# A linear-attention and two-MLP kernel: first token block multiplied in whole fp32, its weights split one block later, its bonus sums taken on TensorE

## The chip, the cores and the metric

One core of one Trainium2 chip. The metric is the device time of one execution in microseconds. Three runs of the kernel before gave 975.14, 975.26 and 977.88 us; the median is 975.26 us.

## What is computed

A linear attention with a decaying state runs over 4 batches, 8 heads, 768 tokens and a head size of 48. Two MLPs (384 to 2048 to 384) follow over all 3072 tokens.

```python
for t in range(S):
    cur = einsum('bhd,bhe->bhde', u * k[t], v[t])
    y[t] = einsum('bhd,bhde->bhe', r[t], state + cur)
    state = w[t][..., None] * state + einsum('bhd,bhe->bhde', k[t], v[t])
x = y as (B*S, 384)
h = x @ w_in;  g = h * clip(h + 3, 0, 6) / 6;  x = g @ w_out       # first MLP
h = x @ w2_in; g = h / (1 + exp(-h));          out = g @ w2_out    # second MLP
```

The weights arrive as 8-byte floats, the rest as 4-byte floats. The part `u * k[t]` of the sum is the bonus: for each token and head it comes to the number sum(r*u*k), by which v[t] is multiplied.

## The kernel before

**Tiling.** The 768 tokens of each batch are cut into 6 chunks of 128. A group is one chunk of one batch, so there are 24 groups, and groups 0 to 3 are the first chunk. A block is one chunk of all 4 batches, 512 tokens. The first MLP takes the blocks in turn (`block1(j)`), then the second does (`block2(j)`). The 2048 hidden features are taken in 16 slices of 128 (`fc`).

**A group of attention** (`attention(g)`). VectorE makes running products of the decay in both directions (`pre`, `suf`), multiplies r and k by them (`rh`, `kh`), and TensorE takes the scores in fp32 (`pa`). VectorE masks them (`a`), TensorE turns `kh` (`pk`), ScalarE copies it (`khn`), and TensorE adds up the outputs in fp32 (`py`) and the growth of the state (`pkv`). For the bonus r, k and v come a second time in natural layout (`nat`, tokens on partitions). L642 and L645 multiply r, u and k into `ruk`, L649 sums it for each head into `bb`, and L658 and L663 scale v into `bv`, which L693 adds to `py`. For groups 0 to 3 VectorE does L642 and L645, and for the others GpSimd. ScalarE copies `py` to `xh`, and VectorE takes what that rounding left as `xl` (L703). The state is copied from `pkv` (L730) and multiplied by the decay over the chunk (L734).

**Weights** (`load_w`). Each `fc` is loaded in 8-byte form (`raw`, two buffers, which also take the decay of groups 2 and 3). VectorE turns it into fp32 in three steps (L32, L38, L44 into `bits`), ScalarE rounds it to the upper part (L495), and VectorE takes the rest as the lower part (L496).

**A product of 128x128 by 128x512** is three matmuls in the faster, less exact form of fp32, called fp32r: upper with upper, upper with lower, lower with upper. `mm1` (L784) does this for three input chunks, `mm2` (L797) for three output chunks, so one `fc` of a block has 6 such products or 18 matmuls, and a block has 96 products. Between them ScalarE and VectorE make `g` (L827, L829) and split it into `gh` (L807 or L808) and `gl` (L810).

**Order.** Every operation is handed to a planner with an engine, a price in ns and a key. The planner goes through time: at each engine it takes what can start first, and among these the smallest key. A buffer of a tag is given out in the order in which the tag's buffers were named. The program then runs each engine in that order. Chunk 0 has keys about -100, the attention of chunk j+1 has those of block j, so it is worked off beside block j. Weight tiles (tag `w`, 16 of them) also serve as temporaries of groups 1 to 3 (called `spare` in the trace).

Of the kernel before, what the change touches and what calls it, by code (L numbers as in the profile page):

```python
# [363 lines left out]
def tile_decay_attention_mlp2(  # L364
# [10 lines left out]
):  # L375

# [63 lines left out]
    u_bc = Part(ap_.tile([128, H, D], F32, name="u_bc"))  # L440
    stray = Part(stray_t)
# [31 lines left out]
    wts = {}  # L473

    def load_w(layer, fc, key, where="wp", after=()):
        src = (m1, m2)[layer]
        nm = f"{layer}_{fc}"
        raw = Part(new("cst", "raw", 2, [128, 2, DM, WW], f"raw{nm}", I32))
        op({"SP": 470}, key - 3, lambda e: e.dma_start(
            out=raw.ap.rearrange("p a f t -> p (a f t)"), in_=src[fc]  # L480
        ), writes=[raw], data=1150.0 * WW, after=after)
        if WW == 2:
            bits = Part(new("cst", "bits", 1, [128, 2, DM], f"bits{nm}", I32))
            val = Part(bits.buf, lambda t: t.bitcast(F32))
# [23 lines left out]
        "a0": (2, 0), "a1": (2, NP * C),  # L508
# [3 lines left out]
    def att(tag, shape, g, sub="", bufs=1):  # L512

        if not (0 < g < B and tag + sub in SPARE):
            return Part(new("ap", tag, bufs, shape, f"{tag}{sub}_{g}"))
        i, off = SPARE[tag + sub]
        if (g, i) not in spare:
            spare[g, i] = new("wp", "w", 16, [128, 4 * DM], f"spare{g}_{i}")
# [12 lines left out]
        return Part(spare[g, i], view)  # L531
# [9 lines left out]
    def load_group(g, key):  # L541
        first = 2 <= g < B

        def home(tag, shape, first_home):
            if not first:
                return Part(new("np", tag, 1 if tag == "rk" else 2, shape, f"{tag}{g}"))
            where, t, bufs, size = first_home
            buf = new(where, t, bufs, [128, size], f"{tag}{g}")
            n = 1
            for x in shape[1:]:  # L550
                n *= x
            return Part(buf, lambda t: t[:shape[0], 0:n].rearrange(
                "p (a b) -> p a b", b=shape[2]) if len(shape) == 3 else t[:shape[0], 0:n])

        ws = home("ws", [PD, SEQ + 1], ("cst", "raw", 2, 4 * DM))
        rk = home("rk", [PD, 2 * NP, C], ("wp", "w", 16, 4 * DM))
        nat = home("nat", [128, 2 * H * D + NP * ED], ("wp", "w", 16, 4 * DM))
        for p, src, data in ((ws, wseq_in, 600.0), (rk, rk_in, 1150.0), (nat, nat_in, 1750.0)):
# [4 lines left out]
        return ws, rk, nat  # L563
# [7 lines left out]
    def attention(g, key):  # L571
# [3 lines left out]
        ws, rk, nat = loads.pop(g) if g in loads else load_group(g, key - 2)  # L575
# [3 lines left out]

        def heads(i):  # L580
            return nat.ap[:, i * H * D:(i + 1) * H * D].rearrange("p (h d) -> p h d", d=D)

        def v():
            return nat.ap[:, 2 * H * D:].rearrange("p (a e) -> p a e", e=ED)
# [45 lines left out]
        if not last:  # L630
# [11 lines left out]
        op({"POOL": 1000} if not first else {"DVE": 560}, key, lambda e: e.tensor_tensor(  # L642
            ruk.ap, heads(0), u_bc.ap, op=ALU.mult
        ), [nat, u_bc], [ruk], port=True)
        op({"POOL": 1000} if not first else {"DVE": 560}, key, lambda e: e.tensor_tensor(  # L645
            ruk.ap, ruk.ap, heads(1), op=ALU.mult
        ), [ruk, nat], [ruk], port=True)
        bb = Part(new("ap", "bb", 2, [128, H, 1], f"bb{g}"))
        op({"DVE": 540}, key, lambda e: e.tensor_reduce(  # L649
            flat(bb), ruk.ap, axis=AX.X, op=ALU.add  # L650
        ), [ruk], [bb])
# [3 lines left out]
        def bonus(e):  # L655
            b = bb.ap.rearrange("p (a i) x -> p a i x", i=2)
            x = v()
# [11 lines left out]
        op({"DVE": 740}, key, bonus, [nat, bb], [bv], port=True)  # L669
# [4 lines left out]
        def outputs(e):  # L674
            x = v()
# [23 lines left out]
           [*a_sb, nat, bv, ident] + ([rh, state] if state else []), [py])  # L699
        xh, xl = x_parts[0, j]  # L700
        sl = slice(o * C, (o + 1) * C)
        op({"ACT": 490}, key, lambda e: e.activation(xh.ap[:, :, sl], py.ap, AF.Copy), [py], [xh])
        op({"DVE": 560}, key, lambda e: e.tensor_tensor(  # L703
            xl.ap[:, :, sl], py.ap, xh.ap[:, :, sl].bitcast(F32), op=ALU.subtract
        ), [py, xh], [xl])

        if not last:
            pkv = att_ps([PD, NP, ED], "pkv", g)

            def outer_kv(e):  # L710
                for p in range(NP):
                    e.matmul(pkv.ap[:, p, :], khn.ap[:, p, :], v()[:, p, :], start=True, stop=True)  # L712

            op({"PE": 700}, key, outer_kv, [khn, nat], [pkv])
# [13 lines left out]
            def first_state(e):  # L728
                for a, b in DENSE:
                    e.tensor_copy(now.ap[:, :, b], pkv.ap[:, :, a])  # L730

            op({"DVE": 760}, key, add_state if state else first_state,
               [pkv, now] if state else [pkv], [now])
            op({"DVE": 560}, key, lambda e: e.tensor_tensor(  # L734
                now.ap.rearrange("p a (i e) -> p a i e", e=T),
                now.ap.rearrange("p a (i e) -> p a i e", e=T),
                grown.ap.to_broadcast([PD, NP, NB, T]), op=ALU.mult,
            ), [now, grown], [now], port=True)
# [33 lines left out]
    def new_x(layer, j):  # L772
        x_parts[layer, j] = tuple(
            Part(new("xp", f"x{i}", 2, [128, KC, N], f"x{i}_{layer}_{j}", F32R)) for i in range(2)
        )

    def mm1(layer, j, fc, key):
        xh, xl = x_parts[layer, j]
        wh, wl = wts[layer, fc]
        h = Part(new("ps", "h", 2, [128, N], f"h{layer}_{j}_{fc}"))  # L780
        for kc in range(KC):
# [9 lines left out]
    def mm2(layer, fc, gh, gl, acc, key):  # L791
        wh, wl = wts[layer, fc]
        for c in range(KC):
            def run(e, c=c):
                sl = slice(c * 128, (c + 1) * 128)
                for i, (a, b) in enumerate(((wh, gh), (wh, gl), (wl, gh))):
# [4 lines left out]
            op({"PE": 681}, key, run, [wh, wl, gh, gl], [acc[c]])  # L801
# [15 lines left out]
    def block1(j, key):  # L817
# [5 lines left out]
        for fc in range(FC):  # L823
            kk = key + fc
            h = mm1(0, j, fc, kk)
            g = Part(new("gp", "g", 2, [128, N], f"g{j}_{fc}"))
# [5 lines left out]
            gh, gl = split(g, f"{j}_{fc}", kk, *engs[j == 0])  # L832
# [24 lines left out]
    def block2(j, key):  # L857
# [25 lines left out]
    MM2 = 1.5  # L883
    loads = {0: load_group(0, FIRST)}
    op({"SP": 470}, FIRST + 0.5, lambda e: e.dma_start(
        out=u_bc.ap.rearrange("p h d -> p (h d)"), in_=u_in
    ), writes=[u_bc], data=550.0)
    loads.update({g: load_group(g, FIRST + g) for g in range(1, B)})
    for j in range(NCH):
# [47 lines left out]
def _layouts(inputs):  # L937
# [33 lines left out]
    nat = np.concatenate([tokens(r), tokens(k), vn.reshape(NG, C, -1)], axis=2)  # L971
# [5 lines left out]
        "wseq": wseq, "rk": rk, "nat": nat,  # L977
# [39 lines left out]
```

## Time and profile before

| | |
|---|---|
| profiled execution | 973.99 us |
| its span, first to last instruction | 972.3 us |
| TensorE matmul busy | 918.6 us (94%) |
| VectorE busy | 589.1 us (61%) |
| ScalarE busy | 274.3 us (28%) |
| GpSimd busy | 46.6 us (5%) |
| mean granted TensorE clock | 0.982 |
| fp32r matmuls of both MLPs (L784, L797) | 3456 |

The span covers the first to the last instruction of the profiled execution; its own time is 1.7 us longer. Matmuls are pipelined and their ends are modelled, so the busy time of TensorE says little of its speed; the distance between starts does. A granted clock of 1.00 is TensorE's level of 2.4 GHz, 0.50 is 1.2 GHz, and a value between them is a mean over time at both.

### The profile page before, as it was taken

What the parts mean: (1) busy time and instruction counts of PE and PEld (TensorE: products, weight loads), DVE (VectorE), ACT (ScalarE), POOL (GpSimd) and SP (SyncE); (2) the same over time, 40 slices, a digit from 0 to 9 for tenths busy, and PEclk for the clock granted to TensorE, in tenths of its full rate; (3) what the DMA queues carried; (4) which work ended last, traced back from release to release, by engine and by line L of the source; (5) the groups of instructions that cost most, each with busy time, mean ns of one, the idle gap of its engine ahead of it and who ended that gap; (6) DMA issues with size and microseconds to landing.
All of it is one profiled execution on the core that took longest, in us unless ns stands there. A gap on an engine that the chain in (4) does not pass through costs nothing.

```text
span 972.3 us, 13210 instructions
## 1 busy us (share of the span) xinstructions
PE 918.6 (94%) x5402; PEld 746.1 (77%) x5402; DVE 589.1 (61%) x995; ACT 274.3 (28%) x483; POOL 46.6 (5%) x53
## 2 busy tenths in 40 slices
PE   3579798999999999999999999999999999999996
PEld 2457576888888888888888888888778888888885
DVE  6789999776667577666447787755552322322222
ACT  0023332222222132221125884334431211211111
POOL 0010110000001010002000000000000000000000
PEclk9879999999999999999999999999999999999999
DMA  9245543322223032121018674587760100100101
GB/s 258 89 152 162 174 167 104 93 79 65 78 64 100 10 117 81 55 78 46 1 37 270 199 248 159 165 305 256 246 228 1 33 1 0 33 1 1 33 1 35
DMA packets 36596, 102.68 MB, mean 106 GB/s; under 512 B 3248, under 2 KB 12592, under 8 KB 36528
## 3 DMA queue, kind: packets, MB, share of 16 engines
q1 hardware_dynamic: 36528, 101.77, 32.6%
q8 instruction: 43, 0.70, 0.3%
q14 instruction: 25, 0.20, 0.1%
HBM read 92.32 MB, written 9.44 MB: 105 GB/s over the span
## 4 chain that ended last, share of the span: by engine, by line
PE 84%; DMA 7%; DVE 6%; ACT 2%; issue 1%; SPq 0%; ACTq 0%
PE h L784 37%; PE acc L797 19%; PE acd L797 18%; DMA craw<-in_moe_w_dram 4%; PE py L679 4%; PE pa L616 3%; PE pkv L712 2%; DMA rk<-in_rk_dram 1%; PE py L693 1%; PE pk L635 1%; DMA nat<-in_nat_dram 1%; ACT cval L28 1%; DVE bits L38 1%; DVE w L496 1%; DVE bits L44 1%
## 5 line engine op out<-in xcount | busy, mean ns | idle before, releaser
L784 PE MATMUL h<-x,w 128*128 128x512 f32 x1728 | 435.7, 394 | 9.6 <-ACT w L495 5.2
L784 PEld LDWEIGHTS h<-x,w 128*128 128x128 f32 x1728 | 322.5, 189 | 82.2 <-DVE w L496 7.9
L797 PE MATMUL acc<-gh,w 128*128 128x512 f32 x576 | 198.8, 397 | 0.0
L797 PE MATMUL acd<-gh,w 128*128 128x512 f32 x576 | 194.1, 392 | 0.4 <-DVE gh L808 0.4
L808 DVE CAST gh<-g 128x512 fp32r<-128x512 f32 x142 | 60.6, 427 | 178.7 <-ACT g L866 175.6
L810 DVE TENSOR_TENSOR gl<-g,gh 128x512 fp32r<-128x512 f32 x192 | 131.9, 687 | 4.8 <-ACT gh L807 0.8
L797 PEld LDWEIGHTS acc<-gh,w 128*128 128x128 f32 x576 | 109.8, 191 | 23.8
L797 PEld LDWEIGHTS acd<-gh,w 128*128 128x128 f32 x576 | 108.2, 188 | 24.7 <-DVE gh L808 1.3
L827 ACT ACTIVATE g<-h 128x512 f32<-128x512 f32 x96 | 57.4, 597 | 239.3 <-PE h L784 239.3
L866 ACT ACTIVATE g<-h 128x512 f32<-128x512 f32 x96 | 57.3, 597 | 226.1 <-PE h L784 220.2
L797 PE MATMUL acc<-gl,w 128*128 128x512 f32 x288 | 114.2, 396 | 5.2 <-DVE gl L810 5.2
L829 DVE SCALAR_TENSOR_TENSOR g<-g,h 128x512 f32<-128x512 f32 x96 | 65.7, 685 | 85.1 <-ACT g L827 84.9
L797 PE MATMUL acd<-gl,w 128*128 128x512 f32 x288 | 113.2, 393 | 0.9 <-DVE gl L810 0.9
L797 PEld LDWEIGHTS acc<-gl,w 128*128 128x128 f32 x288 | 54.9, 191 | 17.8 <-DVE gl L810 6.7
L797 PEld LDWEIGHTS acd<-gl,w 128*128 128x128 f32 x288 | 54.1, 188 | 14.3 <-DVE gl L810 2.5
L766 DVE TENSOR_SCALAR_CACHE_REDUCE cval<-cval 128x768 f32<-128x768 f32 x32 | 30.4, 951 | 31.9 <-ACT cval L28 31.8
L28 ACT ACTIVATE cval<-craw 128x768 f32<-128x768 f32 x32 | 28.8, 899 | 45.2 <-DMA craw<-in_moe_w_dram 39.3
L642 POOL TENSOR_TENSOR ruk<-nat,u_bc 128x384 f32<-128x384 f32 x20 | 20.5, 1027 | 411.6 <-PE py L693 388.0
L807 ACT ACTIVATE gh<-g 128x512 fp32r<-128x512 f32 x50 | 31.3, 628 | 21.9 <-DVE g L829 21.7
L616 PE MATMUL pa<-rh,kh 48*128 48x128 f32 x336 | 26.1, 298 | 10.4 <-DVE kh L606 10.4
L616 PEld LDWEIGHTS pa<-rh,kh 48*128 48x128 f32 x336 | 22.0, 200 | 17.8 <-DVE kh L606 11.1
L496 DVE TENSOR_TENSOR w<-bits,w 128x768 fp32r<-128x768 f32 x32 | 30.5, 952 | 8.3 <-ACT w L495 8.3
(87 smaller groups left out, 633.0 us busy)
## 6 DMA issues: line engine op xcount, KB each, us to landing
raw<-in_moe_w_dram SPq DMA_DIRECT2D x32, 768.0 KB, 4.5
craw<-in_moe_w_dram SPq DMA_DIRECT2D x32, 768.0 KB, 5.1
nat<-in_nat_dram SPq DMA_DIRECT2D x24, 608.0 KB, 3.9
rk<-in_rk_dram SPq DMA_DIRECT2D x24, 448.0 KB, 4.2
ws<-in_wseq_dram SPq DMA_DIRECT2D x24, 226.2 KB, 2.6
cw<-in_wseq_dram SPq DMA_DIRECT2D x24, 226.2 KB, 2.9
x2d<-x SPq DMA_DIRECT2D x18, 256.0 KB, 2.4
xr<-x2d SPq DMA_DIRECT2D x6, 768.0 KB, 7.1
```

The source lines that it names most:

```text
L28: e.activation(val, raw[:, :, :, 1].bitcast(F32), AF.Square)
L496: op({"DVE": 960}, key, lambda e: e.tensor_tensor(lo.ap, val.ap, hi.ap.bitcast(F32), op=ALU.subtract), [val, hi], [lo], port=True)
L616: e.matmul(pa[i].ap[:, p, :], kh.ap[rows, p, :], rh.ap[rows, p, :], start=True, stop=True,)
L679: e.matmul(py.ap[p * Q:(p + 1) * Q, c, :], lhs, rhs, start=p not in begun, stop=False, skip_group_check=True,)
L784: e.matmul(h.ap, a.ap[:, 0, kc * 128:(kc + 1) * 128], b.ap[:, kc, :], start=(kc == 0 and i == 0), stop=(kc == KC - 1 and i == 2),)
L797: e.matmul(acc[c].ap, a.ap[:, 1, sl], b.ap, start=(fc == 0 and i == 0), stop=(fc == FC - 1 and i == 2),)
L807: e.activation(gh.ap, src.ap, AF.Copy) if e is nc.scalar
L808: else e.tensor_copy(gh.ap, src.ap)
L810: op(lo_engs, key, lambda e: e.tensor_tensor(gl.ap, src.ap, gh.ap.bitcast(F32), op=ALU.subtract), [src, gh], [gl], port=True)
L827: op({"ACT": 595}, kk, lambda e, g=g, h=h: e.activation(g.ap, h.ap, AF.Relu, bias=3.0), [h], [g])
L829: op({"DVE": 690}, kk, lambda e, g=g, h=h: e.scalar_tensor_tensor(g.ap, g.ap, 6.0, h.ap, op0=ALU.min, op1=ALU.mult), [g, h], [g])
L866: op({"ACT": 595}, kk, lambda e, g=g, h=h: e.activation(g.ap, h.ap, AF.Silu), [h], [g])
```

## The change

Four things are done for groups 0 to 3 and block 0, and the sizes of some buffers follow.

- Block 0 multiplies whole fp32 values: one fp32 matmul takes the place of three fp32r ones. It needs no `xl`, no `gh`, no `gl`, and no split weights. The fp32 weights stay in weight tiles, two `fc` in one.
- The split of the first MLP's weights into upper and lower parts is a step of its own (`split_w`), named after block 1's own operations, with keys from 13 to 28 (block 1 has 16 to 31).
- The bonus sums of groups 0 to 3 come from r*k in the turned layout (`rkp`) by four small fp32 matmuls with u (`u_bd`, 112 x 2 for each pair of heads) into PSUM. These groups load only v in natural layout (`vn`); groups 4 to 23 also load r and k (`rkn`).
- The first state is taken from `pkv` and multiplied by the decay in the same step.

```diff
@@ load_w
+        if whole:
+            if fc % 2 == 0:
+                vals[fc] = new("wp", "w", WBUFS, [128, 2, 2, DM], f"val{nm}")
+            val = Part(vals[fc - fc % 2], lambda t: t[:, fc % 2])
+            bits = val
...
+        wts[layer, fc] = (val,)
+        if not whole:
+            split_w(layer, fc, key, where)
+
+    def split_w(layer, fc, key, where="wp"):
+        val, = wts[layer, fc]
+        t = new(where, "w" if where == "wp" else "lw", WBUFS if where == "wp" else LATE_W,
+                [128, 2, 2, DM], f"w{layer}_{fc}", F32R)
         hi, lo = Part(t, lambda t: t[:, 0]), Part(t, lambda t: t[:, 1])
         op({"ACT": 850}, key, lambda e: e.activation(hi.ap, val.ap, AF.Copy), [val], [hi])
         op({"DVE": 960}, key, lambda e: e.tensor_tensor(
...
-    LATE_W = 5
-    ALSO_H = ("py", "pk", "pkv")
+    LATE_W = 4
+    ALSO_H = ("py", "pk", "pkv", "bb")
...
+    WBUFS = 17
@@ load_group
-        nat = home("nat", [128, 2 * H * D + NP * ED], ("wp", "w", 16, 4 * DM))
+        vn = home("vn", [128, NP, ED], ("wp", "w", WBUFS, 4 * DM))
+        if g >= B:
+            rkn = Part(new("np", "rkn", 2, [128, 2 * H, D], f"rkn{g}"))
@@ attention
+        if first:
+            rkp = att("rkp", [PD, NP, C], g)
+            op({"DVE": 690}, key, lambda e: e.tensor_tensor(
+                rkp.ap, of(rk, 0, NP), of(rk, 1, NP), op=ALU.mult
+            ), [rk], [rkp], port=True)
+            bb = att_ps([128, H, 1], "bb", g)
+
+            def sums(e):
+                for p in range(NP):
+                    e.matmul(bb.ap[:, 2 * p:2 * p + 2, 0], rkp.ap[:, p, :], u_bd.ap[:, p, :],
+                             start=True, stop=True)
+
+            op({"PE": 900}, key, sums, [rkp, u_bd], [bb])
+        else:
...
+            if state:
+                op({"DVE": 760}, key, add_state, [pkv, now], [now])
...
+            else:
+                op({"DVE": 760}, key, lambda e: scaled(pkv, e), [pkv, grown], [now])
@@ mm1 (mm2 in the same way)
+        if not xl:
+            for kc in range(KC):
+                op({"PE": 860}, key, lambda e, kc=kc: e.matmul(
+                    h.ap, wh.ap[:, 0, kc * 128:(kc + 1) * 128], xh.ap[:, kc, :],
+                    start=kc == 0, stop=kc == KC - 1,
+                ), [wh, xh], [h])
+            return h
@@ the program's order
+    WHOLE = (0,)
...
+    for p, src, k in ((u_bd, ub_in, 0.2), (u_bc, u_in, B + 0.5)):
...
-                load_w(0, fc, fc - 3.0)
+                load_w(0, fc, fc - 3.0, whole=True)
         else:
             block1(j - 1, FC * (j - 1))
+            if j - 1 == max(WHOLE):
+                for fc in range(FC):
+                    split_w(0, fc, FC * (max(WHOLE) + 1) + fc - 3.0)
```

## Rows read from the trace of the kernel before

**Rows 1.** Page, part 2: busy tenths in 40 slices of 24.3 us

```profile
PE   3579798999999999999999999999999999999996
...
DVE  6789999776667577666447787755552322322222
```

**Rows 2.** Windows: stretch, length, busy PE, PEld, DVE, ACT, POOL (count), clock, DMA, GB/s

```profile
0.00:58.78 58.78, 29.59 (x252) 23.36 (x253) 40.90 (x79) 6.16 (x10) 3.79 (x15) 0.85 0.55 158
...
58.78:180.00 121.22, 106.42 (x754) 82.24 (x755) 115.86 (x183) 39.01 (x62) 12.46 (x10) 0.94 0.48 154
...
180.00:260.00 80.00, 80.00 (x620) 65.94 (x619) 51.98 (x93) 18.11 (x31) 8.38 (x8) 1.00 0.22 69
```

**Rows 3.** TensorE's waits: us in total, times, longest us

```profile
PE pa L616 <- DVE spare L606: 14.9, 3, 6.9
...
PE acc L797 <- DVE gl L810: 5.2, 3, 2.5
PE h L784 <- ACT w L495: 5.2, 4, 1.6
PE h L784 <- DVE w L496: 4.4, 6, 1.0
```

**Rows 4.** Groups by line and shape, 0 to 180 us: busy us, mean ns, idle before

```profile
L784 PE MATMUL h<-x,w 128*128 128x512 f32 x171 | 47.7, 417 | 9.6 <-ACT w L495 5.2 <-DVE w L496 4.4
L797 PE MATMUL acc<-gh,w 128*128 128x512 f32 x99 | 36.3, 419 | 0.0
...
L797 PE MATMUL acc<-gl,w 128*128 128x512 f32 x49 | 21.1, 431 | 5.2 <-DVE gl L810 5.2
...
L496 DVE TENSOR_TENSOR w<-bits,w 128x768 fp32r<-128x768 f32 x16 | 15.2, 948 | 1.0 <-ACT w L495 1.0
...
L810 DVE TENSOR_TENSOR gl<-g,gh 128x512 fp32r<-128x512 f32 x18 | 12.3, 682 | 0.0
...
L734 DVE TENSOR_TENSOR s<-s,grown 112x384 f32<-112x384 f32 x9 | 7.7, 850 | 0.0
...
L703 DVE TENSOR_TENSOR x<-py,x 128x384 fp32r<-128x384 f32 x9 | 5.0, 555 | 4.9 <-ACT x L702 4.9
L606 DVE TENSOR_TENSOR kh<-rk,suf 112x512 f32<-112x512 f32 x7 | 4.8, 684 | 0.0
...
L649 DVE TENSOR_REDUCE bb<-spare 128x8 f32<-128x384 f32 x3 | 1.6, 545 | 0.0
L642 DVE TENSOR_TENSOR spare<-nat,u_bc 128x384 f32<-128x384 f32 x3 | 1.6, 544 | 0.0
```

**Rows 5.** Chain that ended last, in time: start us, us, what

```profile
12.05 12.05 DMA rk<-in_rk_dram
...
25.47 2.08 PE pa L616 x16
...
49.28 2.08 PE pa L616 x16
...
169.28 2.04 PE acc L797 x9
...
185.60 1.09 PE pa L616 x16
187.22 2.09 PE acc L797 x9
189.31 0.79 PE pkv L712 x8
190.10 1.67 PE py L679 x56
192.24 2.08 PE h L784 x9
```

**Rows 6.** Weight loads by line and shape, 262 to 428 us

```profile
L784 PEld LDWEIGHTS h<-x,w 128*128 128x128 f32 x287 | 52.9, 188 | 10.5
...
L712 PEld LDWEIGHTS pkv<-nat,khn 128*112 128x112 f32 x56 | 6.3, 177 | 0.3
```

More of the change, by code (lines that the diff above doesn't have):

```diff
@@ L440, in tile_decay_attention_mlp2 @@
     u_bc = Part(ap_.tile([128, H, D], F32, name="u_bc"))
+    u_bd = Part(ap_.tile([PD, NP, 2], F32, name="u_bd"))
     stray = Part(stray_t)
@@ L470, in tile_decay_attention_mlp2, with load_w @@
     op({"DVE": 100}, FIRST, lambda e: e.memset(stray.ap, 0.0), writes=[stray])
-    wts = {}
-    def load_w(layer, fc, key, where="wp", after=()):
+    wts, vals = {}, {}
+    WBUFS = 17
+    def load_w(layer, fc, key, where="wp", after=(), whole=False):
         src = (m1, m2)[layer]
@@ L555, in load_group @@
         ws = home("ws", [PD, SEQ + 1], ("cst", "raw", 2, 4 * DM))
-        rk = home("rk", [PD, 2 * NP, C], ("wp", "w", 16, 4 * DM))
-        nat = home("nat", [128, 2 * H * D + NP * ED], ("wp", "w", 16, 4 * DM))
-        for p, src, data in ((ws, wseq_in, 600.0), (rk, rk_in, 1150.0), (nat, nat_in, 1750.0)):
+        rk = home("rk", [PD, 2 * NP, C], ("wp", "w", WBUFS, 4 * DM))
+        vn = home("vn", [128, NP, ED], ("wp", "w", WBUFS, 4 * DM))
+        parts = [(ws, wseq_in, 700.0), (rk, rk_in, 1400.0), (vn, v_in, 700.0)]
+        rkn = None
+        if g >= B:
+            rkn = Part(new("np", "rkn", 2, [128, 2 * H, D], f"rkn{g}"))
+            parts.append((rkn, rkn_in, 1200.0))
+        for p, src, data in parts:
             op({"SP": 470}, key, lambda e, p=p, src=src: e.dma_start(
@@ L562, in load_group @@
             ), writes=[p], data=data)
-        return ws, rk, nat
+        return ws, rk, vn, rkn
     states = {}
@@ L573, in attention @@
         first, last = g < B, g >= NG - B
-        ws, rk, nat = loads.pop(g) if g in loads else load_group(g, key - 2)
+        ws, rk, vn, rkn = loads.pop(g) if g in loads else load_group(g, key - 2)
         def of(t, i, n):
             return t.ap[:, i * n:(i + 1) * n, :]
[L580 to L584, printed above, removed]
         DENSE = ((slice(0, 2 * Q + T), slice(0, 2 * Q + T)),
@@ L641, in attention @@
         ruk = att("ruk", [128, H, D], g)
[L642 to L651, printed above, removed]
+        if first:
[10 more added lines that the diff above has]
+        else:
+            op({"POOL": 1000}, key, lambda e: e.tensor_tensor(
+                ruk.ap, of(rkn, 0, H), u_bc.ap, op=ALU.mult
+            ), [rkn, u_bc], [ruk], port=True)
+            op({"POOL": 1000}, key, lambda e: e.tensor_tensor(
+                ruk.ap, ruk.ap, of(rkn, 1, H), op=ALU.mult
+            ), [ruk, rkn], [ruk], port=True)
+            bb = Part(new("ap", "bb", 2, [128, H, 1], f"bb{g}"))
+            op({"DVE": 540}, key, lambda e: e.tensor_reduce(
+                flat(bb), ruk.ap, axis=AX.X, op=ALU.add
+            ), [ruk], [bb])
         bv = Part(ruk.buf, lambda t: flat(ruk).rearrange("p (c a e) -> p c a e", c=KC, e=Q))
@@ L667, in bonus @@
             )
-        op({"DVE": 740}, key, bonus, [nat, bb], [bv], port=True)
+        op({"DVE": 740}, key, bonus, [vn, bb], [bv], port=not first)
         state = states.get(o)
@@ L711, in outer_kv @@
                 for p in range(NP):
-                    e.matmul(pkv.ap[:, p, :], khn.ap[:, p, :], v()[:, p, :], start=True, stop=True)
-            op({"PE": 700}, key, outer_kv, [khn, nat], [pkv])
+                    e.matmul(pkv.ap[:, p, :], khn.ap[:, p, :], vn.ap[:, p, :], start=True, stop=True)
+            op({"PE": 700}, key, outer_kv, [khn, vn], [pkv])
             grown = Part(new("ap", "grown", 2, [PD, NP, NB, 1], f"grown{g}"))
@@ L726, in add_state, with scaled @@
                     )
[L728 removed]
+            def scaled(x, e):
                 for a, b in DENSE:
[L730 to L738, printed above, removed]
+                    b = slice(b.start // T, b.stop // T)
+                    e.tensor_tensor(
+                        now.ap.rearrange("p a (i t) -> p a i t", t=T)[:, :, b],
+                        x.ap[:, :, a].rearrange("p a (i t) -> p a i t", t=T),
+                        grown.ap[:, :, b].to_broadcast([PD, NP, b.stop - b.start, T]), op=ALU.mult,
+                    )
+            if state:
+                op({"DVE": 760}, key, add_state, [pkv, now], [now])
+                op({"DVE": 560}, key, lambda e: e.tensor_tensor(
+                    now.ap.rearrange("p a (i t) -> p a i t", t=T),
+                    now.ap.rearrange("p a (i t) -> p a i t", t=T),
+                    grown.ap.to_broadcast([PD, NP, NB, T]), op=ALU.mult,
+                ), [now, grown], [now], port=True)
+            else:
+                op({"DVE": 760}, key, lambda e: scaled(pkv, e), [pkv, grown], [now])
             states[o] = now
@@ L772, in new_x @@
     def new_x(layer, j):
+        whole = layer == 0 and j in WHOLE
         x_parts[layer, j] = tuple(
-            Part(new("xp", f"x{i}", 2, [128, KC, N], f"x{i}_{layer}_{j}", F32R)) for i in range(2)
+            Part(new("xp", f"x{i}", 2, [128, KC, N], f"x{i}_{layer}_{j}", F32 if whole else F32R))
+            for i in range(1 if whole else 2)
         )
     def mm1(layer, j, fc, key):
-        xh, xl = x_parts[layer, j]
-        wh, wl = wts[layer, fc]
+        xh, *xl = x_parts[layer, j]
+        wh, *wl = wts[layer, fc]
         h = Part(new("ps", "h", 2, [128, N], f"h{layer}_{j}_{fc}"))
+        if not xl:
[5 more added lines that the diff above has]
+            return h
+        wl, = wl
+        xl, = xl
         for kc in range(KC):
@@ L791, in mm2 @@
     def mm2(layer, fc, gh, gl, acc, key):
-        wh, wl = wts[layer, fc]
+        wh, *wl = wts[layer, fc]
         for c in range(KC):
+            if not wl:
+                op({"PE": 860}, key, lambda e, c=c: e.matmul(
+                    acc[c].ap, wh.ap[:, 1, c * 128:(c + 1) * 128], gh.ap,
+                    start=fc == 0, stop=fc == FC - 1,
+                ), [wh, gh], [acc[c]])
+                continue
             def run(e, c=c):
                 sl = slice(c * 128, (c + 1) * 128)
-                for i, (a, b) in enumerate(((wh, gh), (wh, gl), (wl, gh))):
+                for i, (a, b) in enumerate(((wh, gh), (wh, gl), (wl[0], gh))):
                     e.matmul(
@@ L800, in run @@
                     )
-            op({"PE": 681}, key, run, [wh, wl, gh, gl], [acc[c]])
+            op({"PE": 681}, key, run, [wh, wl[0], gh, gl], [acc[c]])
     def split(src, nm, key, hi_engs, lo_engs):
@@ L831, in block1 @@
             ), [g, h], [g])
-            gh, gl = split(g, f"{j}_{fc}", kk, *engs[j == 0])
+            gh, gl = (g, None) if whole else split(g, f"{j}_{fc}", kk, *engs[j == 0])
             mm2(0, fc, gh, gl, acc, kk + MM2)
@@ L970, in _layouts @@
         vn[:, :, :, 2 * (Q + i * T):2 * (Q + i * T) + T] = vt[:, :, :, i, Q:]
-    nat = np.concatenate([tokens(r), tokens(k), vn.reshape(NG, C, -1)], axis=2)
+    u_pairs = np.zeros((HO + D, NP, 2), u.dtype)
+    for i in range(2):
+        u_pairs[i * HO:i * HO + D, :, i] = u.reshape(NP, 2, D)[:, i].T
     d = np.arange(H * D).reshape(NP, 2, D)
@@ L976, in _layouts @@
     out = {
-        "wseq": wseq, "rk": rk, "nat": nat,
+        "wseq": wseq, "rk": rk, "vn": vn.reshape(NG, C, -1),
+        "rkn": np.concatenate([tokens(r), tokens(k)], axis=2),
+        "u_pairs": u_pairs.reshape(HO + D, -1),
         "u_rows": np.broadcast_to(u.reshape(1, H * D), (128, H * D)),
```

54 lines of the change are left out of this document (29 added, 25 removed).

## The prediction

> **What bounds the kernel now.** First the busy tenths of TensorE and VectorE over the span [rows 1]. TensorE is at 9 tenths or full from the eighth slice on, that is from about 170 us. The seven slices before it have TensorE at 3 to 9 and VectorE at 6 to 9. So from 170 us on only less work for TensorE would help, and all that this change can win lies before it.
>
> The windows give sizes [rows 2]. From 180 to 260 us TensorE is busy for all of its 80 us. Up to 58.78 us, where the first matmul of block 0 starts, TensorE works for 29.6 us and VectorE for 40.9. From 58.78 to 180 us VectorE works for 115.86 of 121.22 us and TensorE's granted clock is 0.94.
>
> The waits say who is late [rows 3]. In block 0 TensorE waits 5.2 us for `gl`, 5.2 for the upper parts of the weights and 4.4 for the lower parts, 14.8 us together. All three are products of the split. Before block 0 the largest wait is 14.9 us in three times, for the `kh` of groups 1 to 3.
>
> What would the stretch from 58.78 to 180 us cost if TensorE never waited? By 180 us TensorE has run 171 + 99 + 49 = 319 fp32r matmuls [rows 4]. In full flow nine take 2.04 us [rows 5], 0.227 us each, so 72.3 us. Five groups of attention (4 to 8) lie in it too. One takes (187.22 - 185.60) + (192.24 - 189.31) = 4.55 us in full flow, read from the starts in the chain [rows 5]; five take 22.8. Together 95.1 us, and 121.2 were spent. So 26.1 us are lost: 14.8 of waits, the rest the clock (0.06 of 121 us is 7.3) and filling the engine again.
>
> **The change, part by part.** The order of the sum is: the time T0 at which block 0 starts, the work of TensorE from there to what now is 180 us, and the rest, which is 972.3 - 180 = 792.3 us and is not touched.
>
> *T0, the data.* Group 1 is the first to be held up by loading: its `rk` is issued at 12.05 us and lands at 24.1 [rows 5], behind all that was issued before it. `rk` has a single buffer, so it waits for group 0. The sizes follow from the shapes in the code: five `ws` of 232 KB, four `rk` of 459, four `nat` of 623 and `u_bc` of 197 are 5.68 MB. After the change four `vn` of 229 KB stand for `nat`, so 4.11 MB. But the `rkn` of groups 4 and 5 (393 KB each) have two buffers of their own and nothing to wait for, so SP passes them ahead of the blocked `rk`: 4.89 MB. From the first issue at 0.8 us the 23.3 us scale to 20.1 by 4.89 MB and to 16.8 by 4.11. I take the first: `rk` lands at 20.9, 3.2 us earlier. That `rk` is now also read by `rkp` adds about 0.7 us (L606) [rows 4] to its wait, not to the queue ahead of it.
>
> *T0, the three cycles after it.* The scores of group 1 start at 25.47 and those of group 3 at 49.28 us [rows 5], 11.9 us for a group; block 0 starts 9.5 us after the latter. In each group VectorE loses three operations of 0.545 us (the two products and the sum, L642 and L649 stand for them) and `xl` at 0.555, and gains `rkp`, priced as the equal product L606 at 0.684 [rows 4]: 1.5 us less. The first state saves its multiply of 0.85 (L734) [rows 4] but pays something in the two copies that now multiply; I take 0.4 of it, between 0 and 0.85. The wait of VectorE for ScalarE's `xh` goes too (4.9 us in nine times up to 180 us, 0.5 each (L703) [rows 4]). TensorE gains the bonus sums, eight passes of two columns. They cost between 8 times 1.67 / 56 = 0.030 us, the price of a small pass of `py` [rows 5], or 0.24 us, and 8 whole weight loads of 0.188 us [rows 6], or 1.5 us. I take 1.0, nearer to the loads since two columns leave nothing to hide them, but most of it lies in TensorE's own waits of 14.9 us [rows 3], since `rkp` needs only `rk`. So a cycle shrinks by 1.5 to 2.7 us, and by nothing if TensorE's chain at low clock takes over (16 passes of `pa` take 2.08 us at 25.47 us and 1.09 at 185.60 [rows 5]). I take 1.7, three times, 5.1 us. T0 = 58.8 - 3.2 - 5.1 = 50.5 us; the bounds are 46 (3.2 and three times 2.7, and a little more from group 0) and 56 (loading alone).
>
> *Block 0 on TensorE.* 96 products change from three fp32r matmuls, 0.68 us [rows 5], to one in fp32. The nearest fp32 row in full flow is `pkv`: four matmuls with 112 columns appear as eight passes in 0.79 us, 0.099 each [rows 5]. So one fp32 matmul is two recorded passes, each of two columns' time per column: 2 x 112 / 2.4 GHz = 93 ns and 5 ns more. With 512 columns that is 2 x (427 + 5) = 0.864 us. Scaled without a fixed part it is 0.903, and with the excess of an fp32r matmul (227 - 213 = 14 ns) on four passes 0.907. I take 0.87, near the row: 96 x 0.19 = 18.2 us more. The bounds are 17.7 and 21.8.
>
> *Block 0 on VectorE.* Of the 115.86 us, the lower parts of the weights (16 x 0.948 = 15.2 us) and `gl` (16 x 0.682 = 10.9 us) go [rows 4], which leaves 89.8. TensorE now needs 95.1 + 18.2 = 113.3 us for the same stretch. So VectorE is no longer what ends last, and 23 us stay free in it. Into these the planner may put the split for block 1 (15.2 us): 9 of its 16 tiles fit beside the 8 tiles of whole weights (17 in all). What does not fit goes to block 1, where VectorE now works 52 of 80 us [rows 2]; with all of it, 67. ScalarE has 16 rounding copies to move and is at 18 of these 80 us. I price the move at nothing, covered by these free times. If the cover fails, it costs up to 15.2 us.
>
> *What stays lost.* Of the 26.1 us the waits for split products cannot recur. The ramp of block 0 stays: the first `g` must pass ScalarE and VectorE before `mm2` can run, and the clock is low where TensorE has just waited. I take 4 us, bounds 1 and 12.
>
> *Elsewhere.* One weight tile less in the late pool and one more in `wp` cancel: both hold a slice of the second MLP early.
>
> **Sum.** 50.5 + 95.1 + 18.2 + 4 + 792.3 = 960.1 us of span. The profiled execution lasts 1.7 us longer than its span (973.99 for 972.3), and the median of the runs is 1.3 above it (975.26): 963.1, so I say 963 us. Its own range is 956 to 968.
>
> **A rule that speaks against it.** The slices of weights load in 188 ns each for fp32r and in 177 for fp32 with 112 columns [rows 6], so no load stands out beside a pass of 0.43 us. The Trainium skill, "TensorE: Matmul & The Clock Gate", section "Weight-path perf modes — Fast Weight Load (FWL) and DoubleRow", says that weights of 128 columns load quicker by a special mode unless their type is FP32; as an estimate from its factor of up to four, the two loads of a product would take 1.5 us, and the sum would be 963 + 96 x 0.63 = 1024 us. The trace does not bear this out, with 177 ns beside 188; no run here shows fp32 weights of 128 columns under 512 columns.
>
> **Rivals.**
>
> Start not shortened. TensorE's half-clock chain or the added data sets the cycles, T0 is 56 to 58. For it: 3.5 to 7 us of TensorE's time per group at low clock. Against it: TensorE waits for `kh` each time [rows 3]. 963 + 6.5 = 969.5.
>
> The split comes back in block 1. If half of the 15.2 us lands on the path there, or the new order makes TensorE wait by as much, 963 + 7.6 = 970.6. Against it: 28 of 80 us free [rows 2].
>
> The change does not do what it says: other waits in block 0 take the place of those for split products. The steps from 8-byte to fp32 stay with VectorE, and `g` passes two engines with `h` in two buffers. If the whole 26.1 us stay lost, TensorE pays 18.2 us for nothing: 963 + 22 = 985, slower. It decides once more than 16 us of the 26 stay. Against it: all three waits of block 0 [rows 3] name products that are gone.
>
> Weight loads of whole fp32 that don't hide. Each product has two; if they stand between its passes it costs 0.87 + 2 x 0.188 = 1.25 us, and 963 + 96 x 0.376 = 999 us follow. It decides once a product takes 1.00 us: then 96 x 0.32 eat the gains of 8.3 + 26.1 - 4 = 30.4 us. Against it: the eight passes of `pkv` in 0.79 us have their loads among them [rows 5, 6].
>
> **How the numbers follow.** Forecast 0.62, start not shortened 0.13, split in block 1 0.15, waits replaced 0.06, slow loads 0.04. The range of 955 to 971.5 holds the forecast but for its tails, the second case and half of the third, about 0.8. A change of under 0.3% (2.9 us, 972.3 to 978.2) cannot be told from none here. Faster: nearly all of the first two and 0.11 of the third, 0.86. The same: 0.05, from the tails of the third and fourth. Slower: 0.09, the last two but a little.
>
> **What would show it.** Right: block 0's matmuls start at about 50 us; 96 passes of `h` and 96 of `acc` in block 0, about 0.43 us apart; no waits for `gl` or the upper part before 150 us, and block 0's share of TensorE at full clock; the first copy of the accumulator (`x2`) some 10 us earlier; L496 spread over block 0 and block 1 with no wait of TensorE on it. Wrong: `rk` of group 1 landing after 23 us, passes over 0.5 us apart, or idle time of TensorE between 100 and 250 us.

## The result, and the profile after

The changed kernel takes 960.95 us in the median of four runs (958.38 to 962.80), beside 976.25 us for the kernel before. The ratio is 0.984, with a 95% interval of 0.9809 to 0.9871. Run again later (e11 below) it took 958.60 us beside 977.26 for the kernel before, ratio 0.9807 (0.9783 to 0.9832). So it is faster, by 15 and 19 us. The forecast was 963 us, range 955 to 971.5. The profiled execution lasts 962.16 us with a span of 960.4.

The busy tenths of the span after, in 40 slices of 24 us; compare [rows 1]:

```profile
PE   4899999999999999999999999999999999999995
...
DVE  6888897775776677575459878654542323322221
```

TensorE is at 9 tenths or full from the third slice on, where it was from the eighth.

Three windows answer to [rows 2], with the same columns: the time up to block 0 after, block 0 after up to the store of its first output, and the same stretch of the kernel before.

```profile
0.00:47.29 47.29, 30.00 (x285) 25.11 (x285) 33.93 (x65) 5.42 (x9) 3.98 (x15) 0.93 0.57 173
```

```profile
47.29:155.80 108.51, 108.51 (x634) 57.80 (x635) 95.79 (x152) 28.02 (x45) 10.46 (x10) 0.98 0.50 160
```

```profile
58.78:175.38 116.60, 101.80 (x733) 78.43 (x734) 111.38 (x176) 37.43 (x60) 12.46 (x10) 0.94 0.48 154
```

Block 0 starts at 47.29 us instead of 58.78. It takes 108.5 us instead of 116.6, and the window shows no idle time of TensorE in it. VectorE works for 95.8 of these 108.5 us, where it worked for 111.4 of 116.6.

TensorE's waits after, in the columns of [rows 3]:

```profile
PE bb L669 <- DVE rkp L662: 9.0, 1, 9.0
PE pa L634 <- DVE spare L624: 4.7, 2, 4.2
PE acd L856 <- DVE gh L867: 3.7, 4, 1.2
PE acd L856 <- DVE gl L869: 1.6, 6, 0.4
```

The waits for `gl` and for the weights in the first MLP are gone, and the wait for the `kh` of groups 1 to 3 fell from 14.9 us to 4.7. At `acd`, in the second MLP, TensorE waits 5.3 us in this execution, where the kernel before had 1.3; in the second execution of the changed kernel (e11) it is 1.7.

The groups up to 165 us, in the columns of [rows 4], show what an fp32 product is made of and when the weights are split:

```profile
L826 PE MATMUL h<-x,val 128*128 128x512 f32 x96 | 46.0, 616 | 0.6 <-ACT x L734 0.6
L847 PE MATMUL acc<-g,val 128*128 128x512 f32 x96 | 44.2, 592 | 0.0
L826 PEld LDWEIGHTS h<-x,val 128*128 128x128 f32 x96 | 18.6, 199 | 22.7 <-issue 21.7 <-ACT x L734 1.0
...
L515 DVE TENSOR_TENSOR w<-val,w 128x768 fp32r<-128x768 f32 x16 | 14.6, 949 | 0.0
```

Block 0 has 192 passes for its 96 products and its loads (199 ns) take little longer than those of fp32r (188 ns [rows 6]). All 16 splits of the first MLP's weights (L515) stand within 165 us, 15 of them in block 0, the first at 123.0 us.

TensorE's timeline gives the starts of the three cycles, the scores of groups 1 to 3 and then block 0 (start, length, line, operation):

```profile
23.18 2.08 PE L634 MATMUL pa<-spare 48*128 48x128 f32 x16 [4.22 <-DVE spare L624]
...
32.72 1.16 PE L634 MATMUL pa<-spare 48*128 48x128 f32 x16 [0.51 <-DVE spare L624]
...
39.62 1.16 PE L634 MATMUL pa<-spare 48*128 48x128 f32 x16
...
47.29 5.62 PE L826 MATMUL h<-x,val 128*128 128x512 f32 x8 [0.58 <-ACT x L734]
```

The chain in time, as in [rows 5], gives the price of a product:

```profile
59.21 2.58 PE acc L847 x6
61.79 2.58 PE h L826 x6
```

Six passes, three products, take 2.58 us: 0.859 us for a product, where the fp32r form took 0.680.

To follow the gain through the span, one mark in each block will do: SP's store of the first output of blocks 0, 1 and 5. Before:

```profile
175.38 0.35 SPq L839 DMA_DIRECT2D x2d<-x  x1
...
258.65 0.34 SPq L839 DMA_DIRECT2D x2d<-x  x1
...
568.49 0.60 SPq L839 DMA_DIRECT2D x2d<-x  x1
```

After:

```profile
155.80 0.35 SPq L899 DMA_DIRECT2D x2d<-x  x1
...
240.12 0.34 SPq L899 DMA_DIRECT2D x2d<-x  x1
...
550.73 0.35 SPq L899 DMA_DIRECT2D x2d<-x  x1
```

The lead is 19.6 us at the end of block 0, 18.5 at block 1 and 17.8 at block 5, but only 11.9 at the end of the span. So in this pair of executions 8 us of what had been won are lost again: 1.8 in blocks 1 to 5, 4.2 from there to the last matmul (963.79 - 568.49 = 395.3 us before, 950.18 - 550.73 = 399.5 after), and 1.7 behind the last matmul (8.5 us before, 10.2 after). The 4.2 us are not a cost of the change: in the second execution of the changed kernel (e11) the same stretch takes 394.0 us, 1.3 less than before.

### The profile page after: what moved, and what is told of

Its sections match the earlier page's. It is cut to its first block, busy times and chain, and to the rows that moved or that the text cites. A ratio compares the mean times of both kernels' runs of the same rounds, so it can differ in the third digit from the quotient of the medians.

```text
span 960.4 us, 13048 instructions
## 1 busy us (share of the span) xinstructions
PE 927.8 (97%) x5338; PEld 727.4 (76%) x5338; DVE 567.4 (59%) x959; ACT 265.9 (28%) x471; POOL 44.7 (5%) x53
## 4 chain that ended last, share of the span: by engine, by line
PE 88%; DMA 7%; DVE 2%; ACT 1%; issue 0%; POOL 0%; SPq 0%; ACTq 0%
PE h L836 34%; PE acc L856 17%; PE acd L856 17%; DMA craw<-in_moe_w_dram 7%; PE h L826 5%; PE acc L847 4%; PE py L711 4%; PE pa L634 3%; PE pkv L746 2%; PE py L725 1%; ACT cval L28 1%; PE pk L653 1%; DMA rk<-in_rk_dram 0%; PE bb L669 0%; DVE cval L807 0%
## 5 line engine op out<-in xcount | busy, mean ns | idle before, releaser
L836 PE MATMUL h<-x,w 128*128 128x512 f32 x1584 | 395.1, 392 | 0.0
L836 PEld LDWEIGHTS h<-x,w 128*128 128x128 f32 x1584 | 295.6, 188 | 62.4 <-issue 0.5
L856 PE MATMUL acc<-gh,w 128*128 128x512 f32 x480 | 163.5, 392 | 0.0
L856 PEld LDWEIGHTS acc<-gh,w 128*128 128x128 f32 x480 | 90.1, 188 | 19.5
L856 PE MATMUL acc<-gl,w 128*128 128x512 f32 x240 | 93.5, 390 | 0.0
L826 PE MATMUL h<-x,val 128*128 128x512 f32 x96 | 46.0, 616 | 0.6 <-ACT x L734 0.6
L28 ACT ACTIVATE cval<-craw 128x768 f32<-128x768 f32 x32 | 28.7, 897 | 59.5 <-DMA craw<-in_moe_w_dram 53.2
L847 PE MATMUL acc<-g,val 128*128 128x512 f32 x96 | 44.2, 592 | 0.0
L674 POOL TENSOR_TENSOR ruk<-rkn,u_bc 128x384 f32<-128x384 f32 x20 | 20.4, 1020 | 394.8 <-PE py L725 358.0
L826 PEld LDWEIGHTS h<-x,val 128*128 128x128 f32 x96 | 18.6, 199 | 22.7 <-issue 21.7
L847 PEld LDWEIGHTS acc<-g,val 128*128 128x128 f32 x96 | 17.8, 190 | 20.2 <-issue 19.1
```

The source lines that it names most:

```text
L28: e.activation(val, raw[:, :, :, 1].bitcast(F32), AF.Square)
L826: op({"PE": 860}, key, lambda e, kc=kc: e.matmul(h.ap, wh.ap[:, 0, kc * 128:(kc + 1) * 128], xh.ap[:, kc, :], start=kc == 0, stop=kc == KC ...
L836: e.matmul(h.ap, a.ap[:, 0, kc * 128:(kc + 1) * 128], b.ap[:, kc, :], start=(kc == 0 and i == 0), stop=(kc == KC - 1 and i == 2),)
L847: op({"PE": 860}, key, lambda e, c=c: e.matmul(acc[c].ap, wh.ap[:, 1, c * 128:(c + 1) * 128], gh.ap, start=fc == 0, stop=fc == FC - 1,), [ ...
L856: e.matmul(acc[c].ap, a.ap[:, 1, sl], b.ap, start=(fc == 0 and i == 0), stop=(fc == FC - 1 and i == 2),)
```

## The experiments

Two questions were open: which part of the change gives what, and where the 6 us at the end went. Theory A: the start and block 0 are two separate gains, one by work that leaves the start, one by VectorE's relief. The rivals are named in each expectation.

**The start alone (e1) and block 0 alone (e2).** e1 is the changed kernel without whole fp32:

```diff
-    WHOLE = (0,)
+    WHOLE = ()
...
-                load_w(0, fc, fc - 3.0, whole=True)
+                load_w(0, fc, fc - 3.0)
         else:
             block1(j - 1, FC * (j - 1))
-            if j - 1 == max(WHOLE):
-                for fc in range(FC):
-                    split_w(0, fc, FC * (max(WHOLE) + 1) + fc - 3.0)
```

e2 is the kernel before with whole fp32 and the later split, of which this is the order:

```diff
-                load_w(0, fc, fc - 3.0)
+                load_w(0, fc, fc - 3.0, whole=True)
         else:
             block1(j - 1, FC * (j - 1))
+            if j - 1 == max(WHOLE):
+                for fc in range(FC):
+                    split_w(0, fc, FC * (max(WHOLE) + 1) + fc - 3.0)
```

> The changed kernel with block 0 multiplied and split as before (no whole fp32); bonus sums, smaller loads and the fused first state stay. Theory A (two separate gains: the start, and VectorE's relief in block 0): block 0 starts at 48 to 52 us instead of 58.8, TensorE's waits for split products in block 0 come back (12 to 16 us of them), time 965 to 969 us. Rival B (block 0 starts earlier only because whole weights and the missing lower part of x take work from the start): block 0 starts after 56 us and the time is 973 us or more.

> The kernel before with whole fp32 in block 0 and the later split, but bonus sums, loads of r, k, v in natural layout and first state as before. Theory A: block 0 starts at 55 to 58 us (only the lower part of x is gone), no waits of TensorE in block 0, time 965 to 969 us. Rival B: block 0 starts by 51 us and the time is 963 us or less. Rival C (VectorE's relief in block 0 is eaten by the 17 us that fp32 costs): 973 us or more.

e1: 964.76 us, ratio 0.9884 (0.9844 to 0.9923). e2: 969.06 us, ratio 0.9933 (0.9913 to 0.9953). The first matmul of block 0 and TensorE's waits in it, first for e1:

```profile
49.57 0.73 PE L836 MATMUL h<-x,w 128*128 128x512 f32 x2 [0.41 <-ACT w L514]
```

```profile
PE acc L856 <- DVE gl L869: 4.8, 3, 3.3
PE h L836 <- DVE w L515: 4.5, 6, 1.3
PE h L836 <- ACT w L514: 3.0, 4, 1.0
```

Then for e2:

```profile
58.53 3.96 PE L801 MATMUL h<-x,val 128*128 128x512 f32 x8 [1.38 <-DVE val L44]
```

```profile
PE h L801 <- DVE val L44: 1.4, 1, 1.4
```

e1 starts block 0 at 49.6 us and has all three old waits in it, 12.3 us together. e2 starts it at 58.5 us and has one wait of 1.4 us left in it. That start lies just over the range given for it (55 to 58 us), and the time just over its own (965 to 969). The two ratios multiply to 0.982, which is near that of the whole change (0.984 and 0.981). Rivals B and C fall, and theory A holds in the main. The gains, 10.6 us for e1 and 6.3 for e2, come to more than the prediction's parts, 8.3 (3.2 + 5.1) for the start and 3.9 (26.1 - 18.2 - 4) for block 0; part by part they can't be compared, since the missing `xl` counts with the start there and with e2 here. Nor are the two gains wholly apart: up to its first store at 160.74 us e1's block 0 takes 111.2 us, 5.4 less than before, although it has the old form. Its waits for split products are 2.5 us shorter there and the granted clock is 0.97 for 0.94; why it gains this was not tried.

**The split at once (e3).** Each slice is split for block 1 right after it is loaded.

```diff
...
                 load_w(0, fc, fc - 3.0, whole=True)
+                whole_w[fc] = wts[0, fc]
+                split_w(0, fc, fc - 3.0)
         else:
             block1(j - 1, FC * (j - 1))
-            if j - 1 == max(WHOLE):
-                for fc in range(FC):
-                    split_w(0, fc, FC * (max(WHOLE) + 1) + fc - 3.0)
```

The lines left out let block 0 go on using the whole weights (`whole_w`).

> The changed kernel with each weight slice split for block 1 right after it is loaded, not beside the end of block 0. Theory A (VectorE had 23 us free in block 0 and whole fp32 needs no split weights): 960 to 964 us, no wait of TensorE over 1 us in block 0. Rival D (putting the split off is what frees block 0): VectorE is late again, 968 us or more.

966.38 us, ratio 0.9921 (0.9893 to 0.995). That is between the two ranges, and waits of over 1 us are there, against theory A. Block 0 and its waits:

```profile
47.62:161.83 114.21, 108.06 (x636) 57.40 (x637) 98.75 (x155) 28.90 (x45) 10.82 (x10) 1.00 0.46 153
```

```profile
PE acc L847 <- DVE g L889: 2.0, 1, 2.0
PE h L826 <- DVE val L44: 1.6, 1, 1.6
PE pkv L746 <- ACT khn L657: 1.4, 2, 0.7
PE py L725 <- DVE ruk L690: 1.3, 1, 1.3
```

Block 0 takes 114.2 us instead of 108.5. TensorE waits 6.3 us, not for split weights but for whole ones, for `g`, for the bonus and for ScalarE's `khn`. Three of the four lie between 50 and 63 us, where VectorE's order has splits from 48.6 us on and VectorE hardly stands still; its free time comes later, and the late keys of the changed kernel put the split there, from 123 us on. The splits of e3 also take their weight tiles earlier, and that was not tried apart.

**Whole fp32 in block 1 too (e6).**

```diff
-    WHOLE = (0,)
+    WHOLE = (0, 1)
```

> The changed kernel with block 1 in whole fp32 as well. Theory A (whole fp32 pays only where VectorE is late; block 1 is bound by TensorE): 96 products at 0.859 us for 0.680 add 17 us, 976 to 980 us, about the time of the kernel before. Rival E (fp32 also frees something in block 1): 970 us or less.

977.76 us, ratio 1.002 (0.9996 to 1.0043). The first stores of blocks 0 and 1:

```profile
159.09 0.35 SPq L899 DMA_DIRECT2D x2d<-x  x1
...
259.75 0.42 SPq L899 DMA_DIRECT2D x2d<-x  x1
```

Block 1 takes 100.7 us where it took 84.3 in the changed kernel: 16.4 us for 96 products, near the 17 expected. In a block bound by TensorE the fp32 form is a plain loss, and rival E falls.

**The same bytes as before (e10).** Groups 0 to 3 load r and k in natural layout again, and nothing reads them.

```diff
-        rkn = None
-        if g >= B:
-            rkn = Part(new("np", "rkn", 2, [128, 2 * H, D], f"rkn{g}"))
-            parts.append((rkn, rkn_in, 1200.0))
+        rkn = home("rkn", [128, 2 * H, D], ("wp", "w", WBUFS, 4 * DM))
+        parts.append((rkn, rkn_in, 1200.0))
```

> The changed kernel, but groups 0 to 3 still load r and k in natural layout (into buffers that nothing reads), so as many bytes stand ahead of the rk of group 1 as before. Theory A as forecast (the smaller loads are worth about 3 us of the start): block 0 starts at 50 to 52 us, 963 to 966 us. Rival H (the start is set by VectorE and TensorE alone): block 0 starts by 48 us, no more than 1 us over the changed kernel run beside it.

957.75 us, ratio 0.9817 (0.9787 to 0.9848), beside 958.60 us for the changed kernel. VectorE begins on the `rk` of group 1 at 22.43 us, TensorE's scores of group 1 start at 23.78, 0.6 to 0.9 us later than in the two executions of the changed kernel, and block 0 starts at 48.37:

```profile
22.43 0.69 DVE L620 TENSOR_TENSOR spare<-rk,spare 112x512 f32<-112x512 f32 x1
```

```profile
23.78 2.08 PE L633 MATMUL pa<-spare 48*128 48x128 f32 x16 [4.95 <-DVE spare L623]
...
48.37 2.84 PE L825 MATMUL h<-x,val 128*128 128x512 f32 x6 [0.58 <-ACT x L733]
```

So putting the bytes back costs nothing that can be seen in the time. That fits rival H's time and not theory A's, but its start (48.4 us) lies between the ranges of both, and the trace does not bear out that VectorE and TensorE alone set it: `rk` is issued at 14.04 us and takes 8.36 us to land, and VectorE goes on with it at once. Two other things moved with this edit. The planner put the bonus sum of group 4, which stands before the `rh` of group 1 in the changed kernel (next experiment), to 53 us, and the time behind the last matmul is 8.5 us, for 10.2 and 10.0 in the changed kernel. So e10 does not price the smaller loads. What they bring is better read from e8.

**The bonus sum of group 4 held back (e8).** The trace after shows VectorE standing for GpSimd while `rk` of group 1 has already landed (issued at 11.9 us, and no transfer of `rk` in this stretch took over 7.8 us, so by 19.7):

```profile
21.37 0.55 DVE L681 TENSOR_REDUCE bb<-ruk 128x8 f32<-128x384 f32 x1 [1.89 <-POOL ruk L677]
21.84 0.68 DVE L621 TENSOR_TENSOR spare<-rk,spare 112x512 f32<-112x512 f32 x1
```

```diff
-            ), [ruk], [bb])
+            ), [ruk], [bb], after=marks if g == B else ())
```

`marks` is the `kh` of group 3.

> The changed kernel with the bonus sum of group 4 on VectorE held back until group 3 has its kh, so that it no longer stands before the rh of group 1 while GpSimd makes its input. Theory A (VectorE stood 1.9 us for GpSimd with rk of group 1 already landed): block 0 starts 1.5 to 3 us earlier, 957 to 960 us. Rival G (loads or TensorE's low clock set the start): same start, 960 to 962 us.

961.09 us, ratio 0.9814 (0.9778 to 0.985); block 0 starts at 46.8 us. No gain can be told from this in the time, as rival G had it. But here `rk` is what the `rh` of group 1 waits for, so its landing can be read, and the scores that follow:

```profile
18.89 1.04 DVE L624 TENSOR_TENSOR spare<-rk,spare 112x512 f32<-112x512 f32 x1 [0.33 <-DMA rk<-in_rk_dram]
```

```profile
21.38 2.08 PE L639 MATMUL pa<-spare 48*128 48x128 f32 x16 [3.08 <-DVE spare L627]
```

`rk` lands at 18.9 us, and at 19.4 and 18.7 in e9 and e12, which have this edit too. With the old bytes it landed at 22.4 (e10) and 24.1 (the kernel before). The scores of group 1 start at 21.3 to 21.8 us in e8, e9 and e12, for 23.8 in e10, which has no bonus sum of group 4 before them either. So the smaller loads are worth about 2 us in these executions, and in the changed kernel VectorE's wait for GpSimd hides most of it. Not all of the wait comes back in e8: the `rh` and `kh` of group 1 take 1.04 and 1.48 us, for 0.68 each in the changed kernel, while GpSimd works on `ruk` beside them.

**The same program again (e11).**

> The changed kernel itself, beside the others of this call: 959 to 962 us; ratio to the kernel before 0.981 to 0.987 as in its first comparison.

958.60 us, just under the range given, ratio 0.9807 (0.9783 to 0.9832). The starts of the cycles in this execution:

```profile
22.85 2.08 PE L634 MATMUL pa<-spare 48*128 48x128 f32 x16 [4.53 <-DVE spare L624]
...
33.04 2.08 PE L634 MATMUL pa<-spare 48*128 48x128 f32 x16
...
42.83 2.08 PE L634 MATMUL pa<-spare 48*128 48x128 f32 x16
...
51.07 3.94 PE L826 MATMUL h<-x,val 128*128 128x512 f32 x8 [0.58 <-ACT x L734]
```

Block 0 starts at 51.1 us, 3.8 later than in the first execution of the same program. There `pa` took 2.08 us for group 1 and 1.16 for groups 2 and 3; here it took 2.08 us in all three. So TensorE's speed in the start differs between executions of one program. The kernel before varies too. e7 below, run on it, has the same operations up to the second MLP; there `rk` of group 1 lands at 28.1 us instead of 24.1, and block 0 starts 3.9 us later:

```profile
62.71 0.73 PE L784 MATMUL h<-x,w 128*128 128x512 f32 x2 [1.31 <-ACT w L495]
```

**The checks in the second MLP (e7, e9, e12).** Behind the first MLP the kernel reads all weights once more and tests them (`check_weights`: load `craw`, square it on ScalarE at L28, count on VectorE) and the decay too (`check_decay`). One wait of TensorE after, seen on ScalarE, VectorE and TensorE:

```profile
645.40 0.89 ACT L28 ACTIVATE cval<-craw 128x768 f32<-128x768 f32 x1 [2.37 <-DMA craw<-in_moe_w_dram]
646.19 0.58 ACT L926 ACTIVATE g<-h 128x512 f32<-128x512 f32 x1
```

```profile
646.32 0.95 DVE L807 TENSOR_SCALAR_CACHE_REDUCE cval<-cval 128x768 f32<-128x768 f32 x1 [2.29 <-ACT cval L28]
...
647.20 0.42 DVE L867 CAST gh<-g 128x512 fp32r<-128x512 f32 x1
```

```profile
647.67 0.49 PE L856 MATMUL acd<-gh,w 128*128 128x512 f32 x1 [1.23 <-DVE gh L867]
```

ScalarE stands 2.37 us for the data of a check; `g` is next in its order. VectorE stands for ScalarE's part of the check, then counts, and only then rounds `gh`, for which TensorE waits 1.23 us. How much it loses so is best read from the count of matmuls in 200 us around the checks, in the columns of [rows 2]. Before, after, and the second execution of the changed kernel:

```profile
580.00:780.00 200.00, 198.65 (x862) 161.16 (x861) 113.43 (x197) 72.15 (x115) 0.00 (x0) 1.00 0.52 175
```

```profile
562.00:762.00 200.00, 194.76 (x839) 156.40 (x838) 108.09 (x189) 71.13 (x113) 0.00 (x0) 1.00 0.52 171
```

```profile
564.00:764.00 200.00, 198.21 (x863) 161.14 (x862) 110.52 (x192) 72.21 (x114) 0.00 (x0) 1.00 0.50 171
```

In full flow it would be 200 / 0.2267 = 882. So 20 matmuls (4.5 us) are lost before, 43 (9.7 us) after and 19 (4.3 us) in the second execution. The loss is there in both kernels, and its size goes with the execution. The pages show how long the checks' weight loads took to land, in the median: 5.1 us before, 5.7 after and 4.9 in the second execution.

Pacing in e7 and e9 (e9 with e8's edit as well) lets check i load only after slice 16 + 2i of the second MLP:

```diff
-        check_decay(i, begin + 2.5 * i, last_att)
+        check_decay(i, begin + 2.5 * i, [*last_att, paced[FC + 2 * i]])
```

and the same for `check_weights`. e12 has e8's edit too, takes the two kinds of check in turn and orders ScalarE's part later than the load:

```diff
...
+    for i in range(2 * FC):
+        check_weights(i // FC, i % FC, begin + 1 + 2 * i, [*last_att, paced[FC + 2 * i]], [paced[FC + 2 * i + 2]])
+        if i < NG:
+            check_decay(i, begin + 2 + 2 * i, [*last_att, paced[FC + 2 * i + 1]], [paced[FC + 2 * i + 3]])
```

> The changed kernel with the checks of decay and weights paced: check i may load only after product fc = 16 + 2i of the second MLP has been issued to its accumulators, instead of as soon as attention is over. Theory A (the 6 us lost between 600 us and the end come from the checks' loads, which block VectorE and ScalarE in order): TensorE has no wait after block 0, time 955 to 958 us. Rival F (the loss is in the slices of the second MLP's weights, one tile fewer in the late pool): waits between 600 and 700 us stay, 960 to 963 us.

> The kernel before with the same pacing of the checks. Theory A: it had 1.3 us of such waits, so 973 to 975 us. Rival F: no change, 975 to 977 us.

> Both the paced checks and the held-back bonus sum on the changed kernel. Theory A: the two gains add, 952 to 956 us. Rivals F and G: 958 to 962 us.

> The changed kernel with the held-back bonus sum and the checks spread over the second MLP: one weight check for every two slices fc and a decay check between them, and ScalarE's part of a check ordered two slices after its load. Theory A (a check costs TensorE only where it stands in ScalarE's or VectorE's order before its data have landed): no waits of TensorE for gh or gl after 600 us, 950 to 954 us. Rival F (pacing gains nothing beyond the first paced version): 955 us or more.

e7 on the changed kernel: 956.05 us, ratio 0.9782 (0.9755 to 0.981), within theory A's range, but 3.6 us of waits at `acd` stay. On the kernel before: 976.96 us, ratio 0.9999 (0.9976 to 1.0021), no change, as rival F had it. e9: 955.00 us, ratio 0.9776 (0.9747 to 0.9805). The first paced version did not spread the weight checks: they write the same sums as the decay checks and come behind all of them, so most stood together at the end again, and the intervals of e7 and e9 overlap that of the changed kernel in e11. e12: 948.76 us, ratio 0.9718 (0.9692 to 0.9743), clear of all three. In its second MLP there is no wait of TensorE for `gh` or `gl`, and the count of matmuls is full, 884 in 200 us:

```profile
561.00:761.00 200.00, 200.00 (x884) 165.58 (x884) 98.23 (x166) 75.14 (x148) 0.00 (x0) 1.00 0.42 136
```

From the first store of block 5 to the last matmul e12 takes 387.6 us, for 393.1 in e9, which differs from it in the checks alone, 394.0 in e11, 395.3 in the kernel before and up to 399.8 in the other kernels whose checks are as before. So the checks are the cause of the late loss, and rival F falls, since the late pool is as small in e12. By the counts the kernel before loses to them as well, though no run won it back there. Of the 9.8 us between e11 and e12, 6.4 lie in this stretch; 3.3 were there at the first store of block 0 already (154.6 us for 157.9), in the part of the program where e12 has e8's edit and executions of one program differ by as much. e12 is the best version found, 28.5 us under the kernel before run beside it (977.26).

## Why the prediction was right

**T0, 50.5 us forecast, 47.3 and 51.1 measured.** The loads did what was forecast and more: `rk` of group 1 landed by 19.7 us, for 20.9 forecast and 24.1 before. The forecast left out VectorE's wait for GpSimd, whose sum for group 4 stands before the `rh` of group 1 and ends at 21.9 us; so the scores of group 1 start only 2.3 and 2.6 us earlier, for 3.2 forecast. The three cycles took 11.7, 12.1 and 9.5 us before; they take 9.5, 6.9 and 7.7 in the first execution after, which is 9.2 us less, and 10.2, 9.8 and 8.2 in the second, 5.1 us less. The forecast was 5.1. The difference is the speed of TensorE's chain, which the prediction had as a bound: the bonus sums, put at 1.0 us, took 1.0 us beside the fast `pa` and 1.7 to 1.9 beside the slow one. What the bonus sums and the fused first state bring each was not tried apart.

**An fp32 product, 0.87 us forecast, 0.859 measured.** It was read from `pkv`, a row of another shape. 96 of them add 17.2 us instead of 18.2.

**VectorE, 23 us free and the split in them.** Right: 15 of 16 splits lie within block 0 and the window shows no idle time of TensorE there. That an amount of free time is not yet a cover is what e3 shows: with the same work in an earlier order block 0 takes 5.7 us more.

**What stays lost in block 0, 4 us forecast.** It was 0.8: of the 26.1 us, 17.2 pay for fp32 and 8.1 came out as a shorter block. In the second execution block 0 takes 106.8 us, 9.8 less than before, and by the same sum nothing stays lost.

**The rest, 792.3 us, taken as untouched.** This was wrong, by 7.7 us from the end of block 0 in the first execution and by 2.0 in the second. About 1.8 us lie in blocks 1 to 5 and 1.7 and 1.5 behind the last matmul, in both. What is left, 4.2 us more and 1.3 less, is the checks, and it varies between executions: the prediction gave no spread for it. That the span of 960.1 us met 960.4 so closely is luck: 3.2 us too much in T0 and 4.2 in block 0 cancel the 7.7. In the second execution the span was 956.8: T0 0.6 later than forecast, block 0 5.9 shorter, the rest 2.0 longer. The mechanism was right; in the first execution its two gains were put too low, and a rest that was put too short made up for it.

**The rivals.** "Start not shortened" and "waits replaced" fall by the trace. "Slow weight loads" fall too: 199 ns for a load beside 188, between passes of 0.43 us. The rule of the Trainium skill (page "TensorE: Matmul & The Clock Gate", section "Weight-path perf modes — Fast Weight Load (FWL) and DoubleRow") that weights of type FP32 get no quick load shows no price here, where a product takes 0.859 us and not the 1.5 estimated; the measured row decides. "The split comes back in block 1" is at most the 1.1 us that block 1 grew (84.3 us for 83.3).

## What to carry to other kernels

In block 0, where VectorE was late, a costlier form of matmul that spares VectorE work was a gain; in block 1, where TensorE is late, the same form was a loss of its full price. So decide it by stage. Free time on an engine hides moved work only if the order puts the work where that time is, behind what others wait for. An operation that waits for data in an engine's order delays all that stands behind it, so background checks should be ordered after their data, not at their load. And when a part of an edit is taken back to price it, look at what else the planner moves: e10 lost a wait together with the saving that it was to price.

## What was not expected

The time behind the last matmul is 8.5 us before, 8.6 in e2, 8.4 in e7 on the kernel before and 8.5 in e10, but 9.7 to 10.4 in every other kernel. So it goes with the smaller loads of groups 0 to 3 and not with the new bonus sums, which e10 has too. Why, stays open.

The granted clock is no sure guide in the first 50 us: in the second execution of the changed kernel its column reads 1.00 from 20 to 50 us, while `pa` took 2.08 us there, and 1.16 for groups 2 and 3 in the first. So the lengths of `pa` are used here to tell TensorE's speed in the start.

The changed kernel started block 0 at 47.3 us in one execution and at 51.1 in another, the kernel before at 58.8 and 62.7, and the checks cost one program 9.7 us in one execution and 4.3 in another. So a difference of 4 or 5 us between two single traces need not come from an edit.
